# Weights kept as a signed length and an angle to the nearer axis in an S4-convolution kernel

## The chip, the cores and the metric

The kernel runs on one core of a Trainium2 chip. The metric is the device time of one execution in microseconds, as the median of several runs. A profiled execution, with a record of every instruction, is read beside it. The engines are TensorE (PE; its weight loads are PEld), VectorE (DVE), ScalarE (ACT), GpSimd (POOL) and the queue engine SyncE (SP), which only issues transfers here. Each engine executes its own instructions in the order in which they are written.

## The reference, cut to what matters

A block with adaptive layer norm: an S4 convolution on 2048 steps of 512 channels, and a mixer with an MLP behind it. The part of interest is the kernel K of the convolution, a sum over 128 complex modes for each channel:

```
mod = silu(c) @ w_mod                     # six rows of 512: sa, ca, ga, sb, cb, gb
h = layernorm(u) * (1 + ca) + sa
dt = exp(log_dt);  A = A_re + 1j*A_im     # 512 channels x 128 modes
P = exp((dt*A)[:, :, None] * arange(2048))
K = einsum("dn,dnl,dn->dl", C, P, dt*B).real
y = causal_convolution(h, K) + h * Dskip  # by FFT of length 4096
x = u + ga * y;  x = x + gb * mixer(layernorm(x)*(1+cb) + sb)
```

For each mode the product C\*B of two complex numbers is needed as a length and an angle: the angle is added to the phase of P, the length to its magnitude.

## The kernel before, in words

**Preparation** (lines 285 to 408, one instruction stream written by hand, `tc.manual_schedule()`). All phases are held in turns. Tiles have 128 partitions and 512 elements (four blocks of 128 channels by 128 modes). Line 329 makes `la` = dt\*A_re, lines 331 to 333 `tf` = dt\*A_im/2π without its whole turns (`frac`, lines 281 to 283, subtracts the nearest whole number), lines 335 and 336 `t64` = 64·`tf`, again without whole turns. Each such tile is split into a high and a low part for fp32r matmuls (`hi` on ACT, `lo` on DVE, both into the tile `hilo`). `place` (line 322) and `parts` (line 359) are matmuls with 0/1 matrices PA and PB that put the rows where the main loop wants them; ACT copies their results to `TES`, `T0S` and `T1S`. `exps` (line 244) makes the magnitudes of P, with matmuls on TES and CE and five Exp activations on ACT.

**The angle of C\*B.** Lines 347 to 353 make `wr` + i·`wi` = C\*B. Lines 367 and 368 take absolute values, line 370 the larger of the two (`mc`), line 373 the smaller (`mn`), and line 376 the arctangent of their ratio, an angle of an eighth of a circle at most. Lines 388 to 396 bring it to the full circle with three reflections, each by a factor and an offset made from a comparison; line 397 adds 31.5·`tf`. Lines 398 to 402 drop whole turns, split the result and put it into the matmuls of `parts(2, 4)`; line 403 copies their sums to `T1S`. The length is `mc`·cos + `mn`·sin of the small angle (lines 378, 379, 405 to 407), times dt (408).

**Modulation** (`load_mod`, `mod_parts`, `mod_sum`, lines 212 to 231): each of six blocks of `w_mod`, 1 MB, is loaded, multiplied by silu(c) on PE in 32 columns' copies, copied by ACT into the first row of its own tile, summed on PE, and copied by ACT to `modu` or `modg`. Blocks 0 and 1 are handled in the preparation (380 to 384); block 2 at lines 547 to 552. The first three stand in tiles of the pool `up`, two buffers of 1 MB that later hold the rows of u (`load_u`).

**Main loop for K** (lines 540 to 593): 32 steps k. `turns(k, 0)` and `turns(k, 1)` (line 449) are matmuls of T0S and T1S with constants, whose results ACT turns into sine and cosine (tile `tr`). `products` multiplies on DVE, `burst` sums on PE into `kp`, and ACT copies that to `KX` once every two steps. `side` holds what is done between steps: layer norm of u, its first transform, and loads. `KX` is one tile of 128 x 8192 for the whole of K; no step writes to it before the third, and then only to its first columns. In the preparation its last 1024 columns hold `wn` and `ws`. Line 545 transposes `wn`, the weights' length, and ACT copies it to `WN`, which `products(0)` needs by way of `weigh` (line 264).

**Behind the loop** come the spectra, the product, the inverse transform, the mixer and the MLP, with their own order.

**Transfers.** SP issues all loads of the preparation but PA, CE, C0, PB and C1, which POOL issues once A_im is there (line 291).

Of the kernel before, what the change touches and what calls it, by code (L numbers as in the profile page):

```python
# [111 lines left out]
def body(ctx, tc, A):  # L112
# [6 lines left out]
    def act(out, in_, f=AF.Copy, scale=1.0, bias=0.0):  # L119
        return S.activation(out, in_, f, bias=bias, scale=scale)  # L120
# [160 lines left out]
    def frac(x, r):  # L281
        V.tensor_scalar(r, x, MAGIC, MAGIC, op0=OP.add, op1=OP.subtract)
        V.tensor_sub(x, x, r)

    with tc.manual_schedule():
# [16 lines left out]
        V.memset(cst, MAGIC)  # L302
        for r in (32, 96):
            V.memset(cst[r:r + 32], 1.0)
        V.tensor_copy(MG, cst)
        V.memset(cst[:, :384], 0.0)
        for i, (r, v) in enumerate(((0, 1.0), (0, -1.0), (32, 0.25))):
            for q in (r, r + 64):
                V.memset(cst[q:q + 1, i * 128:i * 128 + 128], v)
        V.tensor_copy(ON.rearrange("p a b -> p (a b)"), cst[:, :384])  # L310
        V.tensor_scalar(ld[:, 4:], cT, -1.0, None, op0=OP.mult)
        ex = exp_exact(pp, ld, [128, 8], "dt")
        dt = ex[:, :4]
# [24 lines left out]
        lo(0, tf)  # L338
# [3 lines left out]
        place(TES, 6, PA)  # L342
        place(T0S, 0, PA)
# [9 lines left out]
        V.tensor_add(wi, wi, t1)
# [5 lines left out]
        def parts(i0, i1):  # L359
            for v in range(4):  # L360
                for i in range(i0, i1):
                    T.matmul(px[v // 2][:, v % 2 * 512:v % 2 * 512 + 512], PB[:, v, i], hilo[:, 2 + i],
                             start=(i == 0), stop=(i == 3))

        parts(0, 2)
        ax, ay, mn = cr, br, tmp("mn")
        V.scalar_tensor_tensor(ax, wr, -1.0, wr, op0=OP.mult, op1=OP.max)
        V.scalar_tensor_tensor(ay, wi, -1.0, wi, op0=OP.mult, op1=OP.max)
        mx, mc = tmp("mx"), tmp("mc")
        V.tensor_tensor(mc, ax, ay, op=OP.max)  # L370
        V.tensor_scalar(mx, mc, 1e-37, None, op0=OP.max)
        V.reciprocal(mx, mx)
        V.tensor_tensor(mn, ax, ay, op=OP.min)
        V.tensor_mul(mx, mn, mx)
# [5 lines left out]
        mp = [mod_parts(n) for n in range(2)]  # L380
        for f in mp:
            f()
        for n in range(2):
            mod_sum(n)()
        load_mod(2)
        load_u(0)
        sg, sw, si = la, t0, t1
        V.tensor_tensor(sg, ay, ax, op=OP.is_gt)
        V.tensor_scalar(sg, sg, -2.0, None, op0=OP.mult)
        V.tensor_scalar(sw, wr, 0.0, -2.0, op0=OP.is_lt, op1=OP.mult)  # L390
        V.tensor_scalar(si, wi, 0.0, -2.0, op0=OP.is_lt, op1=OP.mult)
        V.scalar_tensor_tensor(at, sg, 1.0, at, op0=OP.add, op1=OP.mult)
        V.scalar_tensor_tensor(at, sg, -0.125, at, op0=OP.mult, op1=OP.add)
        V.scalar_tensor_tensor(at, sw, 1.0, at, op0=OP.add, op1=OP.mult)
        V.scalar_tensor_tensor(at, sw, -0.25, at, op0=OP.mult, op1=OP.add)
        V.scalar_tensor_tensor(at, si, 1.0, at, op0=OP.add, op1=OP.mult)
        V.scalar_tensor_tensor(at, tf, 31.5, at, op0=OP.mult, op1=OP.add)
        frac(at, rr)
        hi(4, at)
        lo(4, at)  # L400
        parts(2, 4)
        for i in range(2):
            act(T1S.rearrange("p (t v) n -> p v t n", v=4)[:, 2 * i:2 * i + 2],
                px[i].rearrange("p (v t n) -> p v t n", v=2, t=4))
        V.tensor_mul(wn, wn, mc)
        V.tensor_mul(ws, ws, mn)
# [133 lines left out]
    with tc.manual_schedule():  # L540
# [729 lines left out]
```

## Time and profile before

| | |
|---|---|
| median of 3 runs | 716.99 us (715.06 to 717.66) |
| the profiled execution, its own time | 714.44 us |
| its span from first to last instruction | 712.6 us |
| busy share PE, DVE, ACT, POOL | 94%, 71%, 47%, 12% |
| mean granted TensorE clock | 0.994 |

In the rows of the timeline the first two numbers are the start and the length in microseconds from the span's start; the bracket gives how long the engine stood idle before the row, and what ended that. All activations have line 120, that of a helper, so they are told apart by their tiles: "out<-in". A number behind x counts merged instructions. Names such as `tp_t` cut an ending off; `xx` is the PSUM tile of `turns`, `exps` and `parts`, `pu` that of `place` and the modulation.

### The profile page before, as it was taken

The page shows a single profiled execution, that of the slowest core. Times are in us where ns is not written, and L with a number is a line of the kernel's source. Part 1 is how long each engine was busy: PE and PEld are TensorE (multiplying, and loading weights), DVE is VectorE, ACT ScalarE, POOL GpSimd, SP SyncE. Part 2 cuts the span into 40 slices and gives each one's busy share as a digit, 9 for nine tenths or more (in the row PEclk, how much of TensorE's full clock was granted, in tenths as well). Part 3 has the DMA queues.
Part 4 walks back from the last instruction along what each step waited for, and adds up shares of the span by engine and source line. Part 5 has one row for each costly group of instructions (what it writes and reads, how often), then busy time and mean ns, then how long its engine had stood idle before and what let it go on. Part 6 is the DMA issues. An engine that isn't in the chain of part 4 may idle for free.

```text
span 712.6 us, 16838 instructions
## 1 busy us (share of the span) xinstructions
PE 669.5 (94%) x7083; PEld 516.9 (73%) x7083; DVE 506.6 (71%) x847; ACT 335.5 (47%) x549; POOL 86.7 (12%) x191
## 2 busy tenths in 40 slices
PE   2689999999999999998999899999999999999997
PEld 1256555656569665664688889999898988989896
DVE  8889999999996666866988868557464636454422
ACT  3769888889866444533344623314123221212120
POOL 1011211112000000000473100101010000000000
PEclk9899999999999999999999999999999999999999
DMA  8451374653439999874659201011020101111011
GB/s 280 145 144 52 91 218 101 181 139 94 141 75 332 237 301 302 267 241 152 204 176 319 90 22 39 16 45 31 27 63 16 53 22 31 31 30 30 0 30 30
DMA packets 56627, 85.51 MB, mean 120 GB/s; under 512 B 5508, under 2 KB 43400, under 8 KB 54888
## 3 DMA queue, kind: packets, MB, share of 16 engines
q1 hardware_dynamic: 52536, 66.87, 33.2%
q0 software_dynamic: 3136, 16.52, 6.5%
q8 instruction: 56, 0.92, 0.6%
q10 hardware_dynamic: 880, 1.05, 0.5%
q14 instruction: 19, 0.16, 0.1%
HBM read 58.20 MB, written 31.85 MB: 126 GB/s over the span
## 4 chain that ended last, share of the span: by engine, by line
PE 47%; DMA 2%; DVE 2%; ACT 1%; issue 1%; SPq 1%; ACTq 0%; DVEq 0%
PE pm L824 7%; PE pm L825 7%; PE pm L827 7%; PE pa L948 6%; PE pa L940 6%; PE pa L941 6%; PE ph L878 2%; PE ph L879 2%; PE ph L881 2%; PE pT L789 2%; DMA ld<-ZT 1%; DMA GD<-go 1%; PE pT L1138 1%; PE py L721 1%; DMA win<-GD 0%
## 5 line engine op out<-in xcount | busy, mean ns | idle before, releaser
L120 ACT ACTIVATE gh<-pm 128x512 fp32r<-128x512 f32 (+1 forms) x48 | 26.9, 561 | 200.6 <-PE pm L827 200.6
L824 PE MATMUL pm<-nh,w3h 128*128 128x256 f32 (+1 forms) x352 | 85.8, 279 | 0.9 <-ACT nh L120 0.9
L825 PE MATMUL pm<-nh,w3l 128*128 128x256 f32 (+1 forms) x352 | 85.6, 279 | 0.1
L932 DVE TENSOR_TENSOR gl<-gf,gh 128x512 fp32r<-128x512 f32 (+1 forms) x48 | 30.9, 643 | 68.3 <-ACT gf L120 68.3
L940 PE MATMUL pa<-w4h,gh 128*128 128x512 f32 (+1 forms) x176 | 69.6, 395 | 0.0
L941 PE MATMUL pa<-w4l,gh 128*128 128x512 f32 (+1 forms) x176 | 68.9, 392 | 0.0
L824 PEld LDWEIGHTS pm<-nh,w3h 128*128 128x128 f32 (+1 forms) x352 | 65.3, 185 | 2.6 <-ACT nh L120 1.1
L825 PEld LDWEIGHTS pm<-nh,w3l 128*128 128x128 f32 (+1 forms) x352 | 65.2, 185 | 2.2 <-DVE w3l L743 0.5
L827 PE MATMUL pm<-nl,w3h 128*128 128x256 f32 (+1 forms) x352 | 54.8, 277 | 0.0
L948 PE MATMUL pa<-w4h,gl 128*128 128x512 f32 (+1 forms) x176 | 48.1, 390 | 0.8 <-DVE gl L932 0.8
L458 PE MATMUL xx<-MG,ON 64*128 64x512 f32 x160 | 47.0, 389 | 0.0
L459 PE MATMUL xx<-MG,ON 64*128 64x512 f32 x160 | 47.0, 389 | 0.0
L827 PEld LDWEIGHTS pm<-nl,w3h 128*128 128x128 f32 (+1 forms) x352 | 46.6, 185 | 0.2 <-DVE nl L797 0.2
L752 POOL TENSOR_TENSOR rs<-mv,eps_t 128x1 f32<-128x1 f32 (+1 forms) x39 | 11.9, 306 | 278.0 <-DVE mv L758 266.1
L884 DVE TENSOR_TENSOR h<-h,ph 128x512 f32<-128x512 f32 x16 | 11.0, 688 | 45.1 <-PE ph L881 45.1
L476 DVE SCALAR_TENSOR_TENSOR e<-tr,p 128x512 f32<-128x512 f32 x64 | 41.1, 683 | 1.8 <-ACT tr L120 1.8
L120 ACT ACTIVATE z<-pz 128x512 f32<-128x512 f32 x32 | 17.4, 594 | 51.4 <-issue 21.7
L677 DVE TENSOR_TENSOR ma<-pk,us 128x512 f32<-128x512 f32 x32 | 21.9, 686 | 26.8 <-issue 15.8
L508 PEld LDWEIGHTS kp<-e,e 128*32 128x32 f32 x2048 | 30.1, 110 | 12.9 <-issue 7.2
L948 PEld LDWEIGHTS pa<-w4h,gl 128*128 128x128 f32 (+1 forms) x176 | 33.0, 188 | 8.3 <-DVE gl L932 1.2
L485 DVE TENSOR_TENSOR e<-tr,p 128x1024 f32<-128x1024 f32 x32 | 39.0, 1218 | 0.0
L486 DVE TENSOR_TENSOR e<-tr,m 128x1024 f32<-128x1024 f32 x32 | 39.0, 1218 | 0.0
(234 smaller groups left out, 1755.6 us busy)
## 6 DMA issues: line engine op xcount, KB each, us to landing
VU<-vs SPq DMA_DIRECT2D x64, 128.0 KB, 3.2
ld<-VU SPq DMA_DIRECT2D x16, 512.0 KB, 14.1
ZT<-z POOLq DMA_DIRECT2D x15, 512.0 KB, 7.1
ld<-ZT SPq DMA_DIRECT2D x12, 512.0 KB, 5.5
Dw<-in_w POOLq DMA_DIRECT2D x8, 688.0 KB, 4.7
xu<-in_u SPq DMA_DIRECT2D x16, 256.0 KB, 5.7
KX<-in_u SPq DMA_DIRECT2D x16, 256.0 KB, 12.3
GD<-go SPq DMA_DIRECT2D x16, 256.0 KB, 2.5
```

The lines of the kernel that those rows point to most:

```text
L120: return S.activation(out, in_, f, bias=bias, scale=scale)
L458: T.matmul(x[:, :512], la, ma, start=(i == 0), stop=(i == len(ops) - 1))
L459: T.matmul(x[:, 512:], lb, mb, start=(i == 0), stop=(i == len(ops) - 1))
L476: V.scalar_tensor_tensor(e0[:, 1, a], tr[:, 1, 0], 1.0 - 2.0 * a, mg[:, a], op0=OP.mult, op1=OP.mult)
L485: V.tensor_mul(e0[:, 0], tr[:, 0, 0:1].to_broadcast([128, 2, 512]), mg)
L486: V.tensor_mul(e1.rearrange("p r d q -> p r (d q)"), tr[:, :, 1], m1s[0][:, u % 2:u % 2 + 1].to_broadcast([128, 2, 512]))
L824: T.matmul(p, wh[:, k, c], hi[k], start=(k == 0), stop=False)
L825: T.matmul(p, wl[:, k, c], hi[k], start=False, stop=False)
L827: T.matmul(p, wh[:, k, c], lo[k], start=False, stop=(k == 3))
L940: T.matmul(acc[i], gh[:m, e, s], W4h[:m, f], start=(f == 0), stop=False)
L941: T.matmul(acc[i], gh[:m, e, s], W4l[:m, f], start=False, stop=False)
L948: T.matmul(acc[i], gl[:m, e, s], W4h[:m, f], start=False, stop=(f == 10))
```

## The change

It rewrites the preparation; the main loop's arithmetic stays.

- **Angle to the nearer axis.** A predicate `sg` (|wi| > |wr|) is made. Where it holds, `copy_predicated` replaces `wr` by `wi`, and `wi` by -`wr`. The ratio of the new `wi` to the new `wr` has a sign, and its arctangent lies within an eighth of a circle to both sides. Then the angle in turns is that arctangent/2π + 0.25·`sg` + 31.5·`tf`; the half circle goes into the length, which is now signed (`wn`·`wr` + `ws`·`wi`). Two scalar_tensor_tensor (one of them ahead of the arctangent) stand where four comparisons, their scalings and six scalar_tensor_tensor stood. The absolute values, -`wr` and 31.5·`tf` are made by ACT.
- **One table.** A sine of one column (`ws[:, :1]`) stands ahead of the arctangent, so that both are taken from one activation table.
- **Constants on POOL**: the memsets and copies that make `MG` and `ON` move from DVE to POOL. The memset of `DS` moves on DVE behind `frac(tf)`, and its four loads on SP with it.
- **Modulation blocks 0 to 2** are loaded into the first 6144 columns of `KX`, behind FK and DS on SP, and with no tile of `up` in use all of them and both `load_u` are issued together. Their sums (`mod_sum(0)`, `mod_sum(1)`) move behind `turns(0, ...)`, block 2 behind `turns(1, ...)`.
- **Order**: `place(T0S)` moves behind the five exponentials, `parts` go through v within i, and the first copy to T1S is cut in two.

At the start of DVE (`cst` is the scratch from which `MG` and `ON` are made; `dt_...` are the small tiles of the exponential that gives dt), before:

```order
L182 MEMSET sp_91 128x1
L298 MEMSET DS 128x128
L184 MEMSET sp_91 1x1 x4
L302 MEMSET cst 128x512
L304 MEMSET cst 32x512 x2
L305 CAST MG<-cst 128x512
L306 MEMSET cst 128x384
L309 MEMSET cst 1x128 x6
L310 CAST ON<-cst 128x384
L311 TENSOR_SCALAR ld<-cT 128x4
L157 TENSOR_SCALAR dt_k<-ld 128x8
```

and now:

```order
L182 MEMSET sp_91 128x1
L184 MEMSET sp_91 1x1 x4
L307 TENSOR_SCALAR ld<-cT 128x4
L157 TENSOR_SCALAR dt_k<-ld 128x8
L158 TENSOR_SCALAR dt_k<-dt_k 128x8
```

The memsets and casts are gone from DVE, so that its first calculation stands right behind the small memsets. On DVE from the product with the reciprocal to the split of the angle, before:

```order
L374 TENSOR_TENSOR tp_mx<-tp_mn,tp_mx 128x512
L388 TENSOR_TENSOR tp_la<-raw_br,raw_cr 128x512
L389 TENSOR_SCALAR tp_la<-tp_la 128x512
L390 TENSOR_SCALAR tp_t_241<-tp_wr 128x512
L391 TENSOR_SCALAR tp_t_242<-tp_wi 128x512
L392 SCALAR_TENSOR_TENSOR tp_at<-tp_la,tp_at 128x512
L393 SCALAR_TENSOR_TENSOR tp_at<-tp_la,tp_at 128x512
L394 SCALAR_TENSOR_TENSOR tp_at<-tp_t_241,tp_at 128x512
L397 SCALAR_TENSOR_TENSOR tp_at<-tp_tf,tp_at 128x512
L282 TENSOR_SCALAR tp_rr<-tp_at 128x512
L283 TENSOR_TENSOR tp_at<-tp_at,tp_rr 128x512
L320 TENSOR_TENSOR hilo<-tp_at,hilo 128x512
```

(two like L394 left out) and now, from the predicate on:

```order
L379 TENSOR_TENSOR tp_la<-raw_br,raw_cr 128x512
L380 COPY_PREDICATED tp_wr<-tp_la,tp_wi 128x512
L381 SCALAR_TENSOR_TENSOR tp_rc<-tp_mc,tp_wr 128x512
L382 RECIPROCAL tp_rc<-tp_rc 128x512
L383 COPY_PREDICATED tp_wi<-tp_la,raw_ci 128x512
L384 TENSOR_TENSOR tp_rc<-tp_rc,tp_wi 128x512
L385 SCALAR_TENSOR_TENSOR tp_rr<-tp_la,tp_rr 128x512
L316 TENSOR_TENSOR hilo<-tp_t_197,hilo 128x512
L391 SCALAR_TENSOR_TENSOR tp_at<-tp_at_304,tp_rr 128x512
L283 TENSOR_SCALAR tp_t_241<-tp_at 128x512
L284 TENSOR_TENSOR tp_at<-tp_at,tp_t_241 128x512
L316 TENSOR_TENSOR hilo<-tp_at,hilo 128x512
```

Between the arctangent (whose result is `tp_at` before and `tp_at_304` now) and the drop of whole turns one instruction stands where six stood. On ACT from the first constants of `turns` to the first sine of the loop (`tr`), before:

```order
L120 ACTIVATE C1N<-C_106 128x512
L120 ACT_TABLE_LOAD
L120 ACTIVATE tp_at_298<-tp_mx 128x512
L120 ACTIVATE tp_at<-tp_at_298 128x512
L120 ACT_TABLE_LOAD
L120 ACTIVATE KX<-tp_at_298,hpi 128x512
L120 ACTIVATE KX<-tp_at_298 128x512
L120 ACTIVATE xu<-pu 128x512 x2
L120 ACTIVATE modu<-pu 128x512 x2
L120 ACTIVATE hilo<-tp_at 128x512
L120 ACTIVATE T1S<-xx 128x2x4x128 x2
L120 ACTIVATE tr<-xx 128x1024
```

and now:

```order
L120 ACTIVATE C1N<-C_106 128x512
L120 ACT_TABLE_LOAD
L120 ACTIVATE KX<-hpi 128x1
L120 ACTIVATE tp_at_304<-tp_rc 128x512
L120 ACTIVATE KX<-pu 128x512
L120 ACTIVATE hilo<-tp_at 128x512
L120 ACTIVATE KX<-pu 128x512
L120 ACTIVATE KX<-tp_at_304,hpi 128x512
L120 ACTIVATE KX<-tp_at_304 128x512
L120 ACTIVATE T1S<-xx 128x4x128 x2
L120 ACTIVATE T1S<-xx 128x2x4x128
L120 ACTIVATE tr<-xx 128x1024
```

One table load, the copy of the arctangent and both copies to `modu` have left this stretch; one copy of a modulation block (`KX<-pu`, `xu<-pu` before) stands ahead of `hilo<-tp_at`, which two such copies and both to `modu` preceded.

The diff, cut to its core:

```
 def load_mod(n):
-    wmt[n] = (up if n < 3 else wml).tile([128, 4, 512], F32, name="xu" if n < 3 else "wm")
+    wmt[n] = KX[:, n * 2048:n * 2048 + 2048].rearrange("p (a b) -> p a b", a=4) if n < 3 else \
+        wml.tile([128, 4, 512], F32, name="wm")
...
 Y.dma_start(FU, A["FU"].rearrange("p (a b) -> p a b", a=2))
-load_mod(0)
-load_mod(1)
-V.memset(DS, 0.0)
-for j in range(4):
-    Y.dma_start(DS[32 * j:32 * j + 1], A["dk"][j:j + 1])
-Y.dma_start(FK, A["FK"])
-V.memset(cst, MAGIC)
+P.memset(cst, MAGIC)
...
-V.tensor_copy(ON.rearrange("p a b -> p (a b)"), cst[:, :384])
+P.tensor_copy(ON.rearrange("p a b -> p (a b)"), cst[:, :384])
+Y.dma_start(FK, A["FK"])
...
 frac(tf, rr)
+V.memset(DS, 0.0)
+for j in range(4):
+    Y.dma_start(DS[32 * j:32 * j + 1], A["dk"][j:j + 1])
+load_mod(0)
+load_mod(1)
+load_mod(2)
+load_u(0)
+load_u(1)
...
 V.tensor_add(wi, wi, t1)
+ax, ay, nr, t31 = cr, br, ci, rr
+lo(0, tf)
+act(ax, wr, AF.Abs)
+act(nr, wr, scale=-1.0)
+act(ay, wi, AF.Abs)
 exps(0, 0, 5)
+place(T0S, 0, PA)
+act(t31, tf, scale=31.5)
 act(C0N, C0.bitcast(F32), scale=-1.0)
 act(C1N, C1.bitcast(F32), scale=-1.0)
+act(ws[:, :1], hpi, AF.Sin)
...
+parts(range(4), 0)
+mp = [mod_parts(0)]
+sg, mc, rc, at, at0 = la.bitcast(I32), tmp("mc"), tmp("rc"), tmp("at"), tmp("at0")
 V.tensor_tensor(mc, ax, ay, op=OP.max)
+V.tensor_tensor(sg, ay, ax, op=OP.is_gt)
+V.copy_predicated(wr, sg, wi)
+V.scalar_tensor_tensor(rc, mc, 1e-37, wr, op0=OP.is_lt, op1=OP.add)
+V.reciprocal(rc, rc)
+V.copy_predicated(wi, sg, nr)
+V.tensor_mul(rc, rc, wi)
+V.scalar_tensor_tensor(t31, sg, 0.25, t31, op0=OP.mult, op1=OP.add)
+act(at0, rc, AF.Arctan)
+lo(2, t64)
+parts(range(4), 1)
+mp.append(mod_parts(1))
+mp[0]()
+V.scalar_tensor_tensor(at, at0, INV2PI, t31, op0=OP.mult, op1=OP.add)
+frac(at, t0)
+hi(4, at)
+mp[1]()
+lo(4, at)
+parts((0, 1), 2, 3)
+parts((2, 3), 2, 3)
 act(wn, at0, AF.Sin, scale=-1.0, bias=hpi)
 act(ws, at0, AF.Sin)
+for i in range(2):
+    act(T1v[:, i], px[0].rearrange("p (v t n) -> p v t n", v=2, t=4)[:, i])
+act(T1v[:, 2:], px[1].rearrange("p (v t n) -> p v t n", v=2, t=4))
+V.tensor_mul(wn, wn, wr)
+V.tensor_mul(ws, ws, wi)
...
 act(WN, wps)
-late = mod_parts(2)
+ms = [mod_sum(n) for n in range(2)]
 turns(1, 0)
-late()
-late = mod_sum(2)
+for f in ms:
+    f()
 turns(1, 1)
-late()
-load_u(1)
+later.append(mod_parts(2))
+late = [lambda: later.append(mod_sum(2))]
 for k in range(33):
     now, later = later, []
     for f in now:
         f()
     if k + 2 < 32:
         turns(k + 2, 0)
         turns(k + 2, 1)
+    while late:
+        late.pop()()
```

More of the change, by code (lines that the diff above doesn't have):

```diff
@@ L295, in body @@
         Y.dma_start(FU, A["FU"].rearrange("p (a b) -> p a b", a=2))
-        load_mod(0)
-        load_mod(1)
-        V.memset(DS, 0.0)
-        for j in range(4):
-            Y.dma_start(DS[32 * j:32 * j + 1], A["dk"][j:j + 1])
-        Y.dma_start(FK, A["FK"])
-        V.memset(cst, MAGIC)
+        P.memset(cst, MAGIC)
         for r in (32, 96):
-            V.memset(cst[r:r + 32], 1.0)
-        V.tensor_copy(MG, cst)
-        V.memset(cst[:, :384], 0.0)
+            P.memset(cst[r:r + 32], 1.0)
+        P.tensor_copy(MG, cst)
+        P.memset(cst[:, :384], 0.0)
         for i, (r, v) in enumerate(((0, 1.0), (0, -1.0), (32, 0.25))):
             for q in (r, r + 64):
-                V.memset(cst[q:q + 1, i * 128:i * 128 + 128], v)
-        V.tensor_copy(ON.rearrange("p a b -> p (a b)"), cst[:, :384])
+                P.memset(cst[q:q + 1, i * 128:i * 128 + 128], v)
+        P.tensor_copy(ON.rearrange("p a b -> p (a b)"), cst[:, :384])
+        Y.dma_start(FK, A["FK"])
         V.tensor_scalar(ld[:, 4:], cT, -1.0, None, op0=OP.mult)
@@ L337, in body @@
         hi(2, t64)
-        lo(0, tf)
+        place(TES, 6, PA)
         V.tensor_scalar(ex[:, 4:], ex[:, 4:], 1.0, None, op0=OP.add)
@@ L341, in body @@
         V.tensor_mul(scb, ex[:, 4:], cT)
-        place(TES, 6, PA)
-        place(T0S, 0, PA)
         cr, ci, br, bi = (f2(raw[k]) for k in ("cr", "ci", "br", "bi"))
@@ L348, in body @@
         V.tensor_mul(t0, ci, bi)
-        lo(2, t64)
         V.tensor_sub(wr, wr, t0)
@@ L353, in body, with parts @@
         V.tensor_add(wi, wi, t1)
+        ax, ay, nr, t31 = cr, br, ci, rr
[3 more added lines that the diff above has]
+        act(ay, wi, AF.Abs)
         exps(0, 0, 5)
+        place(T0S, 0, PA)
+        act(t31, tf, scale=31.5)
         act(C0N, C0.bitcast(F32), scale=-1.0)
         act(C1N, C1.bitcast(F32), scale=-1.0)
+        act(ws[:, :1], hpi, AF.Sin)
         px = [psx.tile([128, 1024], F32, name="xx") for i in range(2)]
-        def parts(i0, i1):
-            for v in range(4):
-                for i in range(i0, i1):
+        def parts(vs, *js):
+            for i in js:
+                for v in vs:
@@ L378, in body @@
+        mp[1]()
+        lo(4, at)
+        parts((0, 1), 2, 3)
+        parts((2, 3), 2, 3)
         act(wn, at0, AF.Sin, scale=-1.0, bias=hpi)
         act(ws, at0, AF.Sin)
[L380 to L401, printed above, removed]
+        T1v = T1S.rearrange("p (t v) n -> p v t n", v=4)
         for i in range(2):
[L403 to L406, printed above, removed]
+            act(T1v[:, i], px[0].rearrange("p (v t n) -> p v t n", v=2, t=4)[:, i])
+        act(T1v[:, 2:], px[1].rearrange("p (v t n) -> p v t n", v=2, t=4))
```

12 lines of the change are left out of this document (removed).

## The prediction

> **What bounds the kernel now.** I read the page's 40 slices first, then the waits of DVE in the loop for K, then the timelines of DVE, ACT and PE ahead of it. In the slices (each 17.8 us) DVE stands at 9 from slice 3 to slice 11, the loop for K:
>
> ```profile
> PE   2689999999999999998999899999999999999997
> DVE  8889999999996666866988868557464636454422
> ```
>
> PE is at 9 there too, so I asked which of the two waits. DVE's waits from 45 to 225 us:
>
> ```profile
> DVE VK L625 <- PE pz L619: 2.6, 6, 1.6
> DVE KX L537 <- ACT KX L120: 1.5, 1, 1.5
> DVE VK L625 <- PE py L619: 1.0, 5, 0.2
> ```
>
> L625 and L537 lie behind the loop (from 212 us). Inside it DVE never waits: the loop lasts as long as DVE's work, and whatever lets DVE begin it sooner is gained in full at its end. What follows starts from results of the loop, not at a fixed hour. So the question is when the loop's first multiplication, L476, starts. DVE ahead of it:
>
> ```profile
> 1.61 0.48 DVE L302 MEMSET cst<- 128x512 f32 x1 [0.15 <-issue]
> 6.05 0.16 DVE L311 TENSOR_SCALAR ld<-cT 128x4 f32<-128x4 f32 x1
> ...
> 18.50 0.69 DVE L353 TENSOR_TENSOR tp_wi<-tp_wi,tp_t 128x512 f32<-128x512 f32 x1
> 21.62 3.35 DVE L372 RECIPROCAL tp_mx<-tp_mx 128x512 f32<-128x512 f32 x1
> 27.89 0.69 DVE L392 SCALAR_TENSOR_TENSOR tp_at<-tp_la,tp_at 128x512 f32<-128x512 f32 x1
> 31.52 0.69 DVE L397 SCALAR_TENSOR_TENSOR tp_at<-tp_tf,tp_at 128x512 f32<-128x512 f32 x1
> 32.71 0.69 DVE L283 TENSOR_TENSOR tp_at<-tp_at,tp_rr 128x512 f32<-128x512 f32 x1
> 35.34 0.69 DVE L320 TENSOR_TENSOR hilo<-tp_at,hilo 128x512 fp32r<-128x512 f32 x1 [1.94 <-ACT hilo L120]
> 40.53 1.29 DVE L476 SCALAR_TENSOR_TENSOR e<-tr,p 128x512 f32<-128x512 f32 x2 [1.84 <-ACT tr L120]
> 42.19 0.43 DVE L264 TENSOR_TENSOR p<-p,WN 128x256 f32<-128x256 f32 x1 [0.37 <-ACT WN L120]
> ```
>
> and ACT:
>
> ```profile
> 17.89 3.78 ACT L120 ACTIVATE p<-xx 128x1024 f32<-128x1024 f32 x4 [0.21 <-PE xx L257]
> ...
> 22.56 1.05 ACT L120 ACTIVATE C0N<-C 128x1024 fp32r<-128x1024 f32 x1
> 23.51 0.62 ACT L120 ACTIVATE C1N<-C 128x512 fp32r<-128x512 f32 x1
> 24.15 1.28 ACT L120 ACT_TABLE_LOAD   x1
> 26.28 0.63 ACT L120 ACTIVATE tp_at<-tp_mx 128x512 f32<-128x512 f32 x1 [0.85 <-DVE tp_mx L374]
> 28.88 0.72 ACT L120 ACTIVATE KX<-tp_at,hpi 128x512 f32<-128x512 f32 x1
> 30.03 1.06 ACT L120 ACTIVATE xu<-pu 128x512 f32<-128x512 f32 x2
> 34.69 0.62 ACT L120 ACTIVATE hilo<-tp_at 128x512 fp32r<-128x512 f32 x1
> 37.08 1.97 ACT L120 ACTIVATE T1S<-xx 128x1024 fp32r<-128x1024 f32 x2 [1.77 <-PE xx L362]
> 39.40 1.03 ACT L120 ACTIVATE tr<-xx 128x1024 f32<-128x1024 f32 x1 [0.36 <-PE xx L459]
> ```
>
> Read backwards: L476 waits for the first sine `tr` (39.40), that for `turns`, that for T1S (37.08), that for the split of the angle (34.69 on ACT, 35.34 on DVE). DVE has the angle at 33.40, but ACT splits it only at 34.69, because two copies to `modu` stand ahead of it. Behind the arctangent (end 26.91) there are 6 scalar_tensor_tensor from 27.89 to 32.21. DVE works without a pause from 1.6 to 33.4, 4.4 us of it (1.61 to 6.05) on constants that nothing needs before 38.
>
> **The sum, part by part.** I rebuild the time at which the first sine starts.
>
> *Start of DVE.* The constants leave DVE. Its first calculation then waits for cT only. The transfers around it:
>
> ```profile
> ld<-in_ld SPq DMA_DIRECT2D x1, 2.0 KB, 1.7
> raw_ar<-in_ar SPq DMA_DIRECT2D x1, 256.0 KB, 3.1
> raw_bi<-in_bi SPq DMA_DIRECT2D x1, 256.0 KB, 5.7
> xu<-in_wm SPq DMA_DIRECT2D x3, 1024.0 KB, 11.4
> FK<-in_FK SPq DMA_DIRECT2D x1, 64.0 KB, 14.4
> 1.68 0.42 SPq L287 DMA_DIRECT2D cT<-in_c x1
> 4.82 0.51 SPq L289 DMA_DIRECT2D raw_bi<-in_bi x1
> ```
>
> cT is issued at 1.68; with 1.7 us like ld it lands at 3.4, with the 3.1 us of raw_ar at 4.8. I take 4.05, so DVE runs 2.0 us ahead of before (bounds 1.3 and 2.6). raw_bi lands at 4.82 + 5.7 = 10.5 and is first read near 12.8, so the inputs don't stop it. `lo` of tf leaves the stretch up to `wi` (-0.6; such a row takes 0.69 and the next may start a little before its end), the memset of DS joins it (+0.1), and the subtraction for `wr` now directly follows the product it needs, which costs 0.1. `wi` therefore starts at 18.50 - 2.0 - 0.4 - 0.5 = 15.6 and ends at 16.2.
>
> *ACT up to the arctangent.* Ahead of the exponentials stand now |wr|, -wr and |wi| instead of the four copies to T0S and TES of which only TES stays. Each overwrites an input of `wi`, so the last starts at 16.25 and ends at 16.9 (0.63 us, as the copy of such a tile at 26.28). The exponentials start at 16.9 against 17.89 and take the same 4.7 (17.89 to 22.56): 21.6. Then T0S (two copies, 1.6 with their waits for PE, which does these matmuls only now): 23.2; 31.5·tf 0.6; C0N, C1N, table load as before, 1.0 + 0.65 + 1.3 (22.56 to the end of the load at 25.4); the sine of one column 0.2: the arctangent runs from 26.75 to 27.4. That is half a microsecond later than before: ACT takes back there what DVE gained.
>
> *DVE up to the arctangent.* From |wi| (16.9): max, predicate, copy_predicated, scalar_tensor_tensor, reciprocal 3.35, copy_predicated, product: 6 x 0.65 + 3.35 + 0.2 = 7.5, ready at 24.4, 2.3 us ahead of ACT. No row shows a copy_predicated; its neighbours are 0.69 (L283, two inputs of this size) and 3.35 (the reciprocal). I take 0.69, since it moves as many operands and computes less than a reciprocal. At 3.35 each the two cost 5.3, of which 2.3 is hidden.
>
> *Behind the arctangent.* One scalar_tensor_tensor (27.5), whole turns off (28.2 to 29.35, as L397 to L283: 31.52 to 33.40 is 1.9 for the three), split on ACT at 29.4 to 30.0, low part on DVE 30.1 to 30.8. Before, this last row ended at 36.03: the gain is 5.2. It is made of 3.6 (five rows, 27.89 to 31.52), 1.3 (the copies to `modu` ahead of the split, 33.40 to 34.69), 0.8 (the copy by 1/2π, and the wait until 27.89 behind the arctangent), less the 0.5 at which the arctangent is late. The second table load (27.59 before) lay beside DVE's rows; its 1.28 us gives nothing by itself.
>
> *To the first sine.* PE now ends the v = 0, 1 sums at 31.7, but ACT has the copy of modulation block 1 (0.5) and both sines of the angle (0.7 each) ahead of T1S, so it is free at 31.85; two copies of 0.6 and `turns` follow at 33.0 (38.16 before), first sine at 34.2: 5.2 before the 39.40 of now. `mod_sum(0)` and `mod_sum(1)` go between the transposes and `turns(1, 0)`: 2.2 us of PE, plus a wait for WN. The first sine of step 1 then starts at 39.3; DVE wants it at 42.3 (47.68 - 5.2, in the same distance from L476 as now). DVE's work in the loop is unchanged, so nothing there is given back.
>
> *Loads.* SP issues the modulation blocks only behind the four loads of DS, whose memset on DVE now follows `tf`, near 9.7; that makes 11.3 for the first block (in the order before, it stood directly behind FU). With 11.4 us they land at 22.7, at the slowest such row (FK, 14.4) at 25.7. PE wants block 0 at about 23.5 and ACT copies it at 27.4, so 1.4 us on PE and the copy stay free up to a landing at 26. u lands behind three blocks of 1 MB: DVE reads it at 41, 30 us after its issue. Hidden. The other way round, PA, CE, C0 and PB no longer share the first microseconds with 2 MB of w_mod; PE's first matmul waited for PA until 13.09:
>
> ```profile
> 13.09 3.95 PE L326 MATMUL pu<-hilo,PA 128*128 128x512 f32 x8 [13.09 <-DMA PA<-in_PA]
> 38.16 0.50 PE L458 MATMUL xx<-C,T0S 64*128 64x512 f32 x1 [0.18 <-ACT T1S L120]
> ```
>
> If PA stays there, TES comes out at 15.7 and the three absolute values end at 17.5: 0.6 lost. If it lands by 12.5, none. I expect that.
>
> *POOL's constants.* POOL does six instructions on 384 or 512 columns and six of 128 on one partition. A copy of 384 columns takes it 0.50 (first row below), so six of 0.6 and six of 0.2 make about 5 us, done near 14 if they start behind its issues near 9; they are wanted at 33. A price could lie on DVE, beside which this runs:
>
> ```profile
> L846 POOL COPY win<-go 128x384 f32<-128x384 f32 x2 | 1.0, 504 | 0.0
> ```
>
> ```profile
> 47.05 0.19 POOL L150 TENSOR_TENSOR lur<-lum,eps_t 128x1 f32<-128x1 f32 x1 [37.90 <-DVE lum L148]
> 47.87 0.52 POOL L150 TENSOR_TENSOR lur<-lum,eps_t 128x1 f32<-128x1 f32 x1
> ```
>
> One line of POOL takes 0.19 or 0.52: it is held up beside DVE. Whether DVE is held up by POOL no row shows; by the sizes it is 0 to 1.2 us (two copies of about 0.6). I take 0.3. The Trainium skill ("GPSIMD Engine Reference", on the engines' SBUF ports) has DVE and POOL share a port pair as an exclusive lock, where whichever comes second waits for the whole instruction; the stretched POOL row agrees, and by that rule this edit would cost up to the 1.2.
>
> Sum: 5.2 - 0.3 = 4.9. The profiled execution would go from 714.44 to 709.5. It lies 2.55 under the median of the runs, 716.99, so the median would be 716.99 - 4.9 = 712.1.
>
> **Rivals.** *PE's slow clock falls on the first turns* (no 2). The granted clock in stretches:
>
> ```profile
> 21.00:25.00 4.00, 4.00 (x14) 2.69 (x18) 3.93 (x4) 3.80 (x5) 0.00 (x0) 0.61 0.51 186
> 25.00:31.60 6.60, 2.75 (x18) 0.80 (x17) 6.36 (x12) 5.18 (x8) 0.00 (x0) 0.95 0.00 0
> 31.60:35.00 3.40, 2.56 (x3) 0.46 (x2) 1.73 (x3) 1.40 (x3) 0.00 (x0) 0.59 0.33 102
> ```
>
> (the third number from the end is the clock.) It drops behind stretches in which PE works little, and by the sum PE's idle time ends at 30.1, and the turns start at 33. At half rate `turns(0, 0)` takes 2.5 instead of 1.24 (38.16 to 39.40), `turns(0, 1)` and the transposes as much again: WN, for which DVE waits, comes up to 3.1 later. Half of that to all leaves a gain near 2.4: 714.6. Against it: PE is busy from 20.9 to 28.2 now, and idle for 1.9 only. The Trainium skill ("TensorE: Matmul & The Clock Gate", Part 1) has the clock halved after an idle window of about 3.4 us whose phase is free; the stretch of 3.4 us quoted agrees, and that would mean that the phase decides here.
>
> *copy_predicated as slow as a reciprocal* (no 3): gain 4.9 - 3.0 = 1.9, 715.1. For it: no row. Against: what it does.
>
> *The loads come late* (no 4, the other side). ACT copies block 0 ahead of the split of the angle. Should block 0 land at L past 26, the split moves to about L + 1.5 + 1.6 + 1, PE's other matmuls with it; the gain is gone at L near 31 and the kernel slower by 4 at 35: 721. That takes 24 us from issue, against 11.4 to 14.4 in the rows.
>
> *It doesn't do what it says*: the sine and arctangent share no table, 2 loads return ahead of the split: -2.6, so 714.7. The order of ACT shows one load, so I give it no more than what is left over.
>
> **How the numbers follow.** The sum 0.62; slow clock 0.20; copy_predicated or a missing table gain 0.09; late loads 0.04; better than the sum (PA early, PE warm, both ends of the bounds good: 7 us) 0.05. About 0.5%, 3.6 us, can be told from no change. Faster by that: the sum and the better case without their tails, 0.67; within it: 0.28; slower 0.05. The range: the bounds at DVE's start (+0.6, -0.7), PA (-0.6), POOL (+0.3, -0.9) give the likeliest case 710 to 714.3; with the slow clock's whole and the better case it is 709.5 to 716.
>
> **What would show it.** In the profile after: L307 near 4; arctangent near 27; `hilo<-tp_at` within 2.1 us of the arctangent's end; first `tr` near 34; no wait of DVE between the first multiplication and the end of the loop but for WN. Wrong if copy_predicated is over 1.8 us, if the clock is at half in 33 to 36, if ACT waits at `KX<-pu`, or if the loop, begun 5 us sooner, ends less than 4 us sooner.

## The result and the profile after

The changed kernel takes 710.12 us (median of 5 runs, 709.42 to 712.83) beside 716.87 for the kernel before (5 runs, 715.06 to 717.66). The ratio is 0.992, with a 95% interval of 0.9895 to 0.9945. Measured once more on another occasion, beside 18 runs of the kernel before, it gave 711.29 against 715.1, a ratio of 0.9947 (0.9917 to 0.9977). The profiled execution took 710.0 against 714.44, its span 708.2 against 712.6. The prediction was 712.1, a gain of 4.9; the two comparisons give 6.75 and 3.8, the profile 4.4.

The timeline of DVE after the change (start, length, row, and in brackets the idle time ahead and what ended it):

```profile
3.47 0.17 DVE L307 TENSOR_SCALAR ld<-cT 128x4 f32<-128x4 f32 x1 [2.09 <-DMA cT<-in_c]
...
10.08 0.71 DVE L283 TENSOR_SCALAR tp_rr<-tp_t 128x512 f32<-128x512 f32 x1
...
11.43 0.58 DVE L343 TENSOR_SCALAR dt_o<-dt_o 128x4 f32<-128x4 f32 x1
...
14.27 0.99 DVE L352 TENSOR_TENSOR tp_wi<-raw_cr,raw_bi 128x512 f32<-128x512 f32 x1
...
15.89 0.69 DVE L354 TENSOR_TENSOR tp_wi<-tp_wi,tp_t 128x512 f32<-128x512 f32 x1
...
18.61 0.73 DVE L380 COPY_PREDICATED tp_wr<-tp_la,tp_wi 128x512 f32<-128x512 int32 x1
...
24.09 0.69 DVE L384 TENSOR_TENSOR tp_rc<-tp_rc,tp_wi 128x512 f32<-128x512 f32 x1
...
27.93 0.69 DVE L391 SCALAR_TENSOR_TENSOR tp_at<-tp_at,tp_rr 128x512 f32<-128x512 f32 x1 [1.94 <-ACT tp_at L120]
...
35.51 1.29 DVE L475 SCALAR_TENSOR_TENSOR e<-tr,p 128x512 f32<-128x512 f32 x2 [1.16 <-ACT tr L120]
...
207.66 0.46 DVE L536 TENSOR_TENSOR KX<-DS,KX 128x64 f32<-128x64 f32 x2
```

The last two rows are the two ends of the loop for K. It starts at 35.51 (before: 40.53), 5.0 sooner, and DVE begins its last row at 207.66 (before: 211.89), 4.2 sooner; the span is 4.4 shorter. So the gain is made ahead of the loop and most of it is carried through the rest of the kernel. ACT after the change:

```profile
16.62 0.63 ACT L120 ACTIVATE raw_br<-tp_wi 128x512 f32<-128x512 f32 x1
...
25.88 1.28 ACT L120 ACT_TABLE_LOAD   x1
27.18 0.20 ACT L120 ACTIVATE KX<-hpi 128x1 f32<-128x1 f32 x1
27.29 0.61 ACT L120 ACTIVATE tp_at<-tp_rc 128x512 f32<-128x512 f32 x1
...
29.84 0.63 ACT L120 ACTIVATE hilo<-tp_at 128x512 fp32r<-128x512 f32 x1 [1.46 <-DVE tp_at L284]
...
32.02 2.00 ACT L120 ACTIVATE T1S<-xx 128x512 fp32r<-128x512 f32 x3
34.45 1.03 ACT L120 ACTIVATE tr<-xx 128x1024 f32<-128x1024 f32 x1 [0.43 <-PE xx L458]
```

The arctangent starts 1.0 later than before (27.29 against 26.28), the split of the angle 4.85 sooner (29.84 against 34.69). DVE has the ratio at 24.78, 2.5 ahead of the arctangent: ACT is what the arctangent waits for.

### The profile page after: what moved, and what is told of

Same layout as the page of the kernel before. It is cut to its first block, busy times and chain, and to the rows that moved or that the text cites. A ratio compares the mean times of both kernels' runs of the same rounds, so it can differ in the third digit from the quotient of the medians.

```text
span 708.2 us, 16836 instructions
## 1 busy us (share of the span) xinstructions
PE 670.5 (95%) x7083; PEld 518.3 (73%) x7083; DVE 500.1 (71%) x827; ACT 336.0 (47%) x553; POOL 91.5 (13%) x203
## 3 DMA queue, kind: packets, MB, share of 16 engines
q10 hardware_dynamic: 880, 1.05, 0.5%
## 4 chain that ended last, share of the span: by engine, by line
PE 46%; DMA 4%; DVE 2%; ACT 1%; SPq 1%; issue 1%; ACTq 0%; DVEq 0%
PE pm L825 7%; PE pm L826 7%; PE pm L828 7%; PE pa L949 6%; PE pa L941 6%; PE pa L942 6%; PE ph L880 2%; PE ph L882 2%; PE ph L879 2%; DMA GD<-go 2%; PE pT L790 2%; DMA ld<-ZT 1%; DMA w4l<-Dw 1%; PE pT L1139 1%; SPq L738 1%
## 5 line engine op out<-in xcount | busy, mean ns | idle before, releaser
L457 PE MATMUL xx<-MG,ON 64*128 64x512 f32 x160 | 48.1, 397 | 0.0
L458 PE MATMUL xx<-MG,ON 64*128 64x512 f32 x160 | 48.0, 396 | 0.0
```

The costliest lines, as they stand in the source:

```text
L457: T.matmul(x[:, :512], la, ma, start=(i == 0), stop=(i == len(ops) - 1))
L458: T.matmul(x[:, 512:], lb, mb, start=(i == 0), stop=(i == len(ops) - 1))
```

## The experiments

All are read by the same rows as above. "Loop starts" is the start of the first multiplication on DVE (35.5 in the changed kernel, 40.5 before), "split" that of `hilo<-tp_at` on ACT (29.84 and 34.69). What an edit "is worth" is read from these starts. By the times alone the kernels with the constants on DVE, without the sine, with the early loads, with the sums back, with the constants held back and with C0N and C1N on POOL can't be told from the changed kernel: their intervals overlap with those of the changed kernel. The starts scatter too: in a second execution of the changed kernel the arctangent starts at 26.90 and the loop at 35.12, 0.4 sooner than in the first.

**Constants back on DVE.**

```
-P.memset(cst, MAGIC) ... P.tensor_copy(ON...)
+V.memset(cst, MAGIC) ... V.tensor_copy(ON...)
```

> The changed kernel with one part undone: the constants MG and ON are made on DVE again, ahead of its first calculation. In the changed kernel DVE starts at 3.47 us, wi ends at 16.58, the first sine of the loop starts at 34.45 and its first multiplication at 35.51. Theory A (the start of DVE is carried through |wi| and the exponentials to the end): DVE starts near 5.9, 2.4 later, but DVE rows that POOL held up (1.1 us in all: 0.53 and 0.71 for a whole-turn row of 0.43, 0.58 for one of 0.16, 0.99 for one of 0.68) are short again, so wi ends near 17.9 and the first multiplication starts near 36.8, 1.3 later; about 711.4. Rival B (ACT alone is the bound ahead of the arctangent, DVE's start is hidden): no change, 35.5. Rival C (the long DVE rows have nothing to do with POOL and stay): 2.4 later, 37.9.

```profile
5.79 0.16 DVE L307 TENSOR_SCALAR ld<-cT 128x4 f32<-128x4 f32 x1
...
15.78 0.68 DVE L352 TENSOR_TENSOR tp_wi<-raw_cr,raw_bi 128x512 f32<-128x512 f32 x1
...
36.73 1.29 DVE L475 SCALAR_TENSOR_TENSOR e<-tr,p 128x512 f32<-128x512 f32 x2 [1.18 <-ACT tr L120]
```

In this timeline of DVE the loop starts at 36.73, 1.2 later than in the changed kernel; theory A had 36.8. DVE starts 2.3 later, and gets back 1.1, since its rows are short again (0.68 instead of 0.99 for the product of `wi`). Time 711.56, ratio 0.9955 (0.9931 to 0.9979). Moving the constants is worth 1.2 us at the start of the loop, and DVE's start alone would be worth twice that if POOL did not hold DVE up. At the end of the loop only 0.4 of it is seen (208.04 against 207.66), because the loop itself lost 0.8 us in the changed kernel and nothing here.

**No sine ahead of the arctangent.**

```
-act(ws[:, :1], hpi, AF.Sin)
```

> The changed kernel without the sine of one column ahead of the arctangent, so that arctangent and sine come from two tables again and a second table load stands on ACT ahead of the sines of the small angle. Theory A (ACT is the bound between the split of the angle and T1S): the arctangent is 0.1 earlier, the second load of 1.28 us stands on the path to T1S, first sine of the loop near 35.5 instead of 34.45, time about 1.1 us up. Rival B (the load lies beside DVE's and PE's work as the second load did in the kernel before): first sine 34.3, no change.

ACT in this kernel:

```profile
30.98 1.28 ACT L120 ACT_TABLE_LOAD   x1
...
33.43 1.99 ACT L120 ACTIVATE T1S<-xx 128x512 fp32r<-128x512 f32 x3
```

The second load stands in the way of T1S, which starts at 33.43 instead of 32.02; the loop starts at 36.88, 1.4 later. Time 714.0, ratio 0.9969 (0.9945 to 0.9992). Theory A holds. What the same load cost in the kernel before no run shows; there it stood at 27.59 in ACT's row of work ahead of the split, and the split came 1.3 behind DVE's angle (34.69 against 33.40), so that it cost 1.3 at most and not surely nothing.

**Modulation blocks 0 and 1 loaded early.**

```
 Y.dma_start(FU, ...)
+load_mod(0)
+load_mod(1)
...
-load_mod(0)
-load_mod(1)
 load_mod(2)
```

> The changed kernel with the loads of modulation blocks 0 and 1 issued right behind FU again, 4 us earlier on SP, still into K's tile. Theory A (their place matters little): PA lands near 13.0 instead of 12.0, TES is 1 us later, |wr| waits 0.4 us for it, first multiplication at 35.5 to 35.9, time within 0.5 us. Rival B (w_mod in the queues holds up PA, CE and PB, and the move behind them was a main gain): first multiplication 1.5 us later or more, 37.0.

PA lands 1 us later, and nothing follows from it, as theory A says. PE waits for PA, but the loop starts at 35.59 (35.51 and 35.12 in the two executions of the changed kernel, so that a cost of a few tenths can't be excluded):

```profile
13.09 2.05 PE L324 MATMUL pu<-hilo,PA 128*128 128x512 f32 x4 [13.09 <-DMA PA<-in_PA]
```

Time 710.31, ratio 0.9936 (0.9909 to 0.9962).

**Modulation sums back ahead of the split.**

```
 frac(at, t0)
-hi(4, at)
 mp[1]()
+for n in range(2):
+    mod_sum(n)()
+hi(4, at)
...
-ms = [mod_sum(n) for n in range(2)]
```

> The changed kernel with the sums of modulation blocks 0 and 1 and their copies to modu ahead of the split of the angle again, as in the kernel before. Theory A (the copies to modu ahead of the split were 1.3 us of the gain): PE does the sums from 28.6 to 30.9, the split starts near 31.5 instead of 29.84, first sine near 36.1, first multiplication near 37.2, 1.7 later; about 711.8. Rival B (ACT's other work ahead of T1S hides it): 35.5 as in the changed kernel.

ACT in this kernel:

```profile
26.91 0.61 ACT L120 ACTIVATE tp_at<-tp_rc 128x512 f32<-128x512 f32 x1
27.43 1.09 ACT L120 ACTIVATE KX<-pu 128x512 f32<-128x512 f32 x2
29.22 0.60 ACT L120 ACTIVATE modu<-pu 128x512 f32<-128x512 f32 x1 [0.70 <-PE pu L229]
30.08 0.60 ACT L120 ACTIVATE modu<-pu 128x512 f32<-128x512 f32 x1 [0.26 <-PE pu L229]
30.57 0.62 ACT L120 ACTIVATE hilo<-tp_at 128x512 fp32r<-128x512 f32 x1
```

The split starts 3.66 behind the arctangent's start instead of 2.55: the sums, and the copy of block 1 that this order also puts ahead of the split, cost 1.1 there. The arctangent itself came 0.4 sooner in this execution, so that the loop starts at 36.23, 0.7 later than in the first execution of the changed kernel, and 1.1 later than in its second, whose arctangent starts at the same time (26.90). The direction is theory A's, the size two thirds of its 1.7: PE had both sums done at 30.0, not 30.9. Time 710.58, ratio 0.994 (0.9917 to 0.9963).

**The angle's arithmetic alone, in the kernel before.** The changed lines from the absolute values to `frac(at)` were put into the kernel before; all else stays there.

> The kernel before with the new angle alone: predicate, copy_predicated, signed ratio, the absolute values, -wr and 31.5*tf on ACT; constants, tables, loads and modulation stay as before. Theory A (the five rows less on DVE are worth nothing while ACT has more to do ahead of the arctangent and the copies to modu ahead of the split): |wi| ends at 19.9, the exponentials at 24.6, the arctangent at 28.7 instead of 26.9, both table loads, sines and modulation copies follow, the split starts near 36.0 instead of 34.69, first multiplication near 41.8 instead of 40.53; about 718, slower by 1.3. Rival B (each part gives its own share): the angle's five rows give 3.6 us alone, first multiplication near 37, about 713.3.

ACT in this kernel:

```profile
28.17 0.63 ACT L120 ACTIVATE tp_at<-tp_rc 128x512 f32<-128x512 f32 x1
...
31.27 1.06 ACT L120 ACTIVATE xu<-pu 128x512 f32<-128x512 f32 x2
33.06 0.60 ACT L120 ACTIVATE modu<-pu 128x512 f32<-128x512 f32 x1 [0.73 <-PE pu L228]
33.92 0.60 ACT L120 ACTIVATE modu<-pu 128x512 f32<-128x512 f32 x1 [0.26 <-PE pu L228]
34.41 0.62 ACT L120 ACTIVATE hilo<-tp_at 128x512 fp32r<-128x512 f32 x1
```

The loop starts at 40.25, 0.3 sooner than before; time 714.42 against 715.39, ratio 0.9984 (0.9959 to 1.0009). Both theories had another number. Rival B falls: the rows saved on DVE give nothing by themselves, since the split waits in ACT's own row of work, the last of it the copies to `modu`, which end at 34.5 (before: 34.8). Theory A had the mechanism, but was 1.6 too slow for the split (34.41 against 36.0): it took over from the kernel before the 3.6 us between the copies to `xu` and the split, where PE's clock was at half from 31.0 to 34.4; in this execution it was full throughout and that stretch 2.1. The sums of the modulation on PE, first in the kernel before, then here:

```profile
30.66 3.50 PE L228 MATMUL pu<-xu,sp 128*128 128x512 f32 x4 [3.85 <-ACT xu L120]
```

```profile
31.90 1.98 PE L228 MATMUL pu<-xu,sp 128*128 128x512 f32 x4 [2.02 <-ACT xu L120]
```

So the 0.3 sooner is probably the clock's doing: at the clock of the kernel before these sums would have taken 1.5 longer, and the new angle alone would have started the loop some 1.2 later (an estimate from these two rows: 40.25 + 1.5 against 40.53). No second execution of either kernel was profiled.

**The angle's arithmetic undone alone, in the changed kernel.** The old lines from the absolute values to `frac(at)` (three comparisons with their factors and six scalar_tensor_tensor among them) were put into the changed kernel, which keeps its table, its loads and its order.

> The changed kernel with the arithmetic of the angle undone alone: absolute values, minimum, clamp and the six scalar_tensor_tensor on DVE as in the kernel before, the copy by 1/2pi on ACT; constants, loads, one table, modulation and the order stay as changed. Theory A (behind the arctangent the chain runs on DVE, ahead of it on ACT): ACT has no absolute values and no 31.5*tf, so the exponentials start near 15.5 and the arctangent near 25.2 instead of 27.29; then the copy, a split of t64 and six rows of 0.72 on DVE end near 31.1, the split of the angle starts near 32.3 instead of 29.84, first multiplication near 37.9, 2.4 later than 35.51; about 712.5. Rival B (the rows are hidden as in the kernel before with the new angle alone, where they gave 0.3): 35.5 to 36. Rival C (they cost their whole 3.6 and the copy 0.7): 39.8.

```profile
25.31 0.61 ACT L120 ACTIVATE tp_at<-tp_rr 128x512 f32<-128x512 f32 x1
...
32.16 0.63 ACT L120 ACTIVATE hilo<-tp_at 128x512 fp32r<-128x512 f32 x1 [5.09 <-DVE tp_at L284]
...
34.96 1.09 ACT L120 ACTIVATE T1S<-xx 128x512 fp32r<-128x512 f32 x2 [0.55 <-PE xx L369]
```

In this timeline of ACT the arctangent starts at 25.31 and the split at 32.16, as theory A has them (25.2 and 32.3). So in this setting the angle's arithmetic gives 2.3 us: ACT now waits 5.1 us for DVE. The loop, though, starts at 39.40 and not at 37.9. PE's granted clock in the same execution shows where the other 1.5 come from (windows; the third number from the end is the clock):

```profile
31.00:34.00 3.00, 1.16 (x3) 0.92 (x4) 1.87 (x4) 1.84 (x4) 0.00 (x0) 0.50 1.03 224
34.00:38.00 4.00, 4.00 (x15) 2.73 (x15) 2.59 (x4) 2.52 (x4) 0.00 (x0) 0.54 0.33 74
```

Half the clock to almost 38: PE's sums for T1S (3.78 us instead of 2.39) and the first `turns` ran at half rate. The clock had fallen at 27.4, behind a stretch (25 to 28) in which PE was busy for 1.29 of 3.00 us. Time 714.79, ratio 0.9985 (0.996 to 1.0009).

**POOL's constants held back.**

```
+P.tensor_copy(gate[:, 1:2], wi[:, 0:1])
 P.memset(cst, MAGIC) ...    # moved behind V.tensor_add(wi, wi, t1)
```

> The changed kernel with POOL's constants held back until wi is there (a copy of one column of wi on POOL ahead of them). Theory A (POOL's constants held DVE up by 1.1 us ahead of wi): the whole-turn rows take 0.43 each, the small row 0.16, the product 0.68, wi ends near 15.5 instead of 16.58, the first sine starts near 33.4 instead of 34.45, first multiplication near 34.5; POOL's rows then stand beside the reciprocal's stretch, where DVE has 2.5 us to spare. Rival B (the long rows are not POOL's doing): wi at 16.58 and 35.5 as in the changed kernel.

DVE and, in the last row, its first multiplication:

```profile
9.88 0.43 DVE L283 TENSOR_SCALAR tp_rr<-tp_t 128x512 f32<-128x512 f32 x1
...
10.95 0.16 DVE L334 TENSOR_SCALAR dt_o<-dt_o 128x4 f32<-128x4 f32 x1
...
13.38 0.68 DVE L343 TENSOR_TENSOR tp_wi<-raw_cr,raw_bi 128x512 f32<-128x512 f32 x1
...
14.70 0.69 DVE L345 TENSOR_TENSOR tp_wi<-tp_wi,tp_t 128x512 f32<-128x512 f32 x1
...
35.28 1.29 DVE L476 SCALAR_TENSOR_TENSOR e<-tr,p 128x512 f32<-128x512 f32 x2 [2.12 <-ACT tr L120]
```

The three long rows take 0.43, 0.16 and 0.68 (changed kernel: 0.71, 0.58, 0.99), `wi` starts 1.2 sooner, and so do the arctangent (26.10) and the split (28.66). This far theory A holds to the tenth. Most of the gain, 1.0 of 1.2, was lost to PE again, whose clock fell to half for part of both these windows:

```profile
28.00:31.00 3.00, 1.66 (x4) 1.22 (x5) 1.90 (x3) 2.25 (x4) 0.00 (x0) 0.75 1.00 224
31.00:34.00 3.00, 3.00 (x13) 1.66 (x12) 2.09 (x4) 2.05 (x3) 0.00 (x0) 0.68 1.02 224
```

The means of 0.75 and 0.68 are half the clock from 29.5 to 32.9. PE's sums for T1S took 3.66 us there instead of 2.39. Time 710.19, ratio 0.9945 (0.9922 to 0.9969).

**C0N and C1N on POOL.**

```
-act(C0N, C0.bitcast(F32), scale=-1.0)
-act(C1N, C1.bitcast(F32), scale=-1.0)
+P.tensor_scalar(C0N, C0.bitcast(F32), -1.0, None, op0=OP.mult)
+P.tensor_scalar(C1N, C1.bitcast(F32), -1.0, None, op0=OP.mult)
```

> The changed kernel with the negated constants C0N and C1N made by POOL instead of ACT. Theory A (ACT is the bound up to the arctangent, DVE has the ratio 2.5 us sooner): ACT loses 1.57 us of work ahead of the arctangent, which starts near 25.7 instead of 27.29, first sine near 33.0 instead of 34.45 and first multiplication near 34.0, 1.5 sooner; less up to 0.5 if POOL's rows hold DVE up beside the ratio. Rival B (DVE's ratio is the bound): no change, 35.5.

The arctangent starts at 26.60, 0.7 sooner than in the first execution of the changed kernel (0.3 sooner than in the second), and the loop at 34.81. POOL needs 2.80 for C0N (ACT 1.05) and starts it beside the sum for `wi`. One row of ACT, one of DVE:

```profile
26.60 0.61 ACT L120 ACTIVATE tp_at<-tp_rc 128x512 f32<-128x512 f32 x1
```

```profile
15.94 1.41 DVE L354 TENSOR_TENSOR tp_wi<-tp_wi,tp_t 128x512 f32<-128x512 f32 x1
```

That row took 0.69 without POOL. Of the 1.57 us that ACT lost, 0.75 came back this way. That is theory A's mechanism, but more than the 0.5 that it allowed for (it had 34.0 to 34.5), and the price fell on `wi`, not beside the ratio. Time 709.46, ratio 0.992 (0.9896 to 0.9944).

**Both edits on POOL**, run twice.

> The changed kernel with both: POOL's constants behind wi and C0N, C1N on POOL. Theory A (both gains add as long as DVE's ratio, ready near 24, is ahead of ACT): first sine near 32.0, first multiplication near 33.0, 2.5 sooner than in the changed kernel, about 707.6. Rival B (POOL's rows, now all beside the ratio, hold DVE up there by 2 us and more): the arctangent waits for the ratio, first multiplication near 34.5.

> Both edits on POOL (constants behind wi, C0N and C1N) once more, beside the changed kernel. First multiplication near 32.9; the loop ends near 204.6, 3 us ahead of the changed kernel; ratio to the kernel before near 0.989 by the theory that the start of the loop decides. Its first profile ended late (711.2) because PE stood 3.5 and 1.1 us in the spectra at 251 and 270 us without any wait on another engine; if that is the instruction transfer's chance and not the edit's, a second profile has a span near 705.5; by the rival that POOL's later work shifts the spectra, it has 709 or more again.

DVE in the second of them:

```profile
14.67 0.69 DVE L345 TENSOR_TENSOR tp_wi<-tp_wi,tp_t 128x512 f32<-128x512 f32 x1
...
33.07 1.29 DVE L476 SCALAR_TENSOR_TENSOR e<-tr,p 128x512 f32<-128x512 f32 x2 [1.13 <-ACT tr L120]
...
204.81 0.47 DVE L537 TENSOR_TENSOR KX<-DS,KX 128x64 f32<-128x64 f32 x2
```

The loop starts at 32.88 and 33.07, and ends at 204.61 and 204.81, 2.9 sooner than in the changed kernel. DVE has the ratio at 23.81 and 24.00, still 0.8 ahead of the arctangent (24.60 and 24.80), so that rival B falls. Theory A holds in both. Times 706.39 and 707.51, ratios 0.9873 (0.9818 to 0.9927) and 0.9885 (0.9856 to 0.9914): this version beats both kernels (the changed kernel had 711.29 beside the second). The spans of the two profiles, 711.2 and 705.3, differ, so the late end of the first isn't the edit's doing; more of it below.

**The changed kernel again**, beside the last of these.

> The changed kernel once more, beside the others of this chip. First multiplication at 35.5, the loop's last on DVE ends 4.2 to 5.0 us before the 211.89 of the kernel before; ratio to the kernel before between 0.991 and 0.995 by the theory that the time moves with the start of the loop (5.0 of 717 is 0.993). The rival that the 6.75 us between the first medians hold a second gain behind the loop would have 0.989 to 0.991 again.

The loop starts at 35.12 and ends at 207.34 (4.55 sooner than before). The ratio of 0.9947 is a gain of 3.8 us, with 1.6 to 5.9 in its interval, so that it agrees with the 4 to 5 at the loop; the 0.989 to 0.991 of a second gain behind the loop lie outside.

## Why the prediction was right

The forecast was faster by 4.9, and the path by which it comes about holds: DVE's start, ACT ahead of the arctangent, the split, T1S, the first sine. Two things do not: the price of POOL's constants, and the way in which the gain is divided among the parts.

- **Bound.** "Inside the loop DVE never waits" held nearly: from its start to its end DVE takes 171.4 us before, 172.2 after, and 171.3 to 172.5 in every other kernel here whose loop starts between 32.9 and 40.3. So a start that is 5.0 sooner gave 4.2 at the end, not all of it. The 0.8 lost are three quarters of a microsecond of waits, which the prediction's list of signs had excluded, in DVE's list from 38 us on:

```profile
DVE xu L425 <- DVE xu L424: 0.5, 1, 0.5
DVE e L475 <- ACT tr L120: 0.2, 1, 0.2
```

- **Start of DVE.** Taken at 4.05, it was 3.47; the gain there is 2.6, the upper bound.
- **POOL's constants.** Taken at 0.3, they cost 1.0 to 1.1, near the upper bound of 1.2 (in the second execution of the changed kernel 0.9). This is the term that was mis-sized; that the better start of DVE made up for two thirds of it is luck. By the rule of the Trainium skill that the prediction set beside it ("SBUF — State Buffer", section "Who interferes with whom"; the prediction names another page of the skill), DVE and POOL block each other for whole instructions. The trace agrees: held-back constants give DVE its short rows back. In the changed kernel DVE rows with two tiles as inputs stayed at 0.69 beside POOL's memsets (at 12.33, for example), and the one that was stretched, 0.99 at 14.27, stands beside POOL's cast of `ON` (13.96 to 14.72).
- **ACT ahead of the arctangent.** Forecast start 26.75, measured 27.29: `wi` ends 0.4 late by the former two. That DVE has 2.3 us to spare there (2.5) and that ACT takes back there what DVE gained is confirmed: with the constants held back, C0N and C1N off ACT brought the arctangent from 26.10 to 24.60 and 24.80.
- **copy_predicated** costs 0.73 and 0.69, as taken; its rival falls.
- **Behind the arctangent.** Forecast 2.65 from the start of the arctangent to that of the split, measured 2.55. First sine 34.2 forecast, 34.45 measured; first multiplication 5.0 sooner, of a sum of 4.9.
- **Where the sum divides its gain** it was less good. It gave 3.6 to the five rows and 1.3 to the sums, and nothing to the table load. Undone one at a time in the changed kernel they are worth 2.3, 1.1 and 1.4, the constants 1.2 and the place of the loads 0.1 or a little more. That these add to more than 5.0, and that the angle alone gave nothing in the kernel before, is one thing: DVE's rows on one side, the table load and the copies to `modu` on ACT's lay beside each other, so that fewer rows on DVE brought nothing while ACT's stood. For the table load and the copies, taken away alone in the kernel before, this is argued and not run. The 1.3 at `modu` has a clock in it as well: the kernel before was profiled once, with PE at half clock from 31.0 to 34.4, and its sums at full clock, 1.5 us shorter, would have left DVE's angle (33.40) as the last. So up to 1.3 of the 5.0 may belong to that execution; whether it does in other runs of the kernel before isn't known.
- **Loads.** PA lands at 12.03 (forecast: by 12.5) and ACT never waits at `KX<-pu`. The rival of late loads falls.
- **Slow clock.** The rival did not come true in the changed kernel, where PE had its full clock from 31.6 to 36. The clock did fall ahead of the loop in three of its relatives. With the constants held back and with the old angle it cost about 1 to 1.5 us, of the 2.5 to 3.1 given; in the kernel without the sine (0.50 from 31 to 34) it cost nothing, since T1S waited for ACT's table load anyway. No run shows that the change keeps the clock up there; that both profiled executions of the changed kernel were spared may be luck.

The size of the time itself, 710.12 against 712.1, lies within what single sets of runs scatter: the kernel before had 716.87 in one set and 715.1 to 715.4 in the others. The bounds that the prediction names add up to 711.2 at the lower end of its likeliest case, not to 710, so that 710.12 lies just outside that sum, and within the wider range by its margin.

## What to carry to other kernels

Find the engine that never waits in the long stage, and then only the start of that stage counts; follow the chain that leads to it backwards through all engines, and charge each row where it stands alone on the chain. Work that lies side by side on two engines has to be taken from both, or nothing comes of it: here new arithmetic that saves five rows gave 0.3 us alone, probably by the clock, but 2.3 at the split together with the rest. Work given to POOL isn't free for DVE while DVE is on the path; put it where DVE has slack.

## What was not expected of the hardware

**Where runs of one kernel differ.** The same kernel, with both edits on POOL, ended its loop at 204.6 and 204.8, yet its spans are 711.2 and 705.3. Up to the fifth of the sixteen steps of the spectra (40 us behind the loop's last row) the two executions run alike to 0.4; by the ninth step, some 25 us on, one has fallen back by 6. PE stands there without a wait on any engine, first in the execution of 711.2, then in that of 705.3 (waits of PE from 245 to 275 us):

```profile
PE pk L668 <- issue: 3.5, 1, 3.5
PE pk L645 <- issue: 1.1, 1, 1.1
```

```profile
PE pk L668 <- issue: 0.4, 1, 0.4
```

Transfers keep the queues busy there all the time (their share is 1.06 from 245 to 275 in the former). The record of the packets has one of 16 KB of the instruction queue about every seven to eleven microseconds, and each of these waits ends shortly behind the landing of one: PE goes on at 251.32 and 270.02 where such packets landed at 249.83 and 268.61; in the changed kernel at 269.51 behind 268.14, in the kernel before at 248.33 and 273.26 behind 246.88 and 271.91. That is 1.35 to 1.49 us in these five cases; two more, 265.57 in the execution of 705.3 and 260.88 in the changed kernel, have 1.50. Behind the wait of 3.5 us PE's clock was at half as well (0.51 from 271.0 to 274.5), which makes up for the rest of the 6. That PE waited for its own instructions is likely from this, but no run changed it, so it stays an inference. It is why differences of 1 us between kernels were better read from the start and the end of the loop than from their medians.

**PE's clock fell in a busy stretch.** In the changed kernel, three windows of 3.4 us around 77 us:

```profile
70.40:73.80 3.40, 2.95 (x71) 1.79 (x70) 3.40 (x5) 3.37 (x4) 0.00 (x0) 1.00 0.59 125
73.80:77.20 3.40, 3.06 (x11) 1.55 (x12) 3.25 (x6) 3.19 (x4) 0.03 (x1) 1.00 0.00 0
77.20:80.60 3.40, 3.40 (x18) 2.28 (x14) 3.40 (x5) 3.21 (x5) 1.94 (x3) 0.51 0.42 142
```

PE was busy 3.06 of the 3.40 us ahead of it, no less than in the window before that, and its clock was halved all the same. The Trainium skill ("TensorE: Matmul & The Clock Gate", Part 1) ties this to a window of idleness, and the busy share in the record doesn't bear that out here. About half of the work in that window are the matmuls of `exps` on 32 of the 128 rows; whether the chip counts those as less work no run here decides. In the kernel with the early loads the same rows stand 0.12 us later, PE is busy for the same 3.06, and the clock stays at 1.00 from 77.2 to 80.6, so that this work alone doesn't decide it. The half clock cost the loop a wait of a quarter of a microsecond (at 81.96), which the executions without it don't have.

**POOL is slow at simple products.** A product of 128 x 1024 elements with a constant took POOL 2.80 us (partly beside DVE, which it held up) and ACT 1.05, though copies of 128 x 384 take POOL 0.50.
